# A fused attention and gated MLP kernel on one core: the opening in another order, merged exponentials, and row sums moved to TensorE

## The chip, the core and the metric

The kernel runs on one core of a Trainium2 chip. The metric is device time in microseconds for one execution; the kernel before has been run three times, and the profile is one further execution of it. Five engines with their own instruction streams work side by side: TensorE (PE in the profile, with PEld for its weight loads), VectorE (DVE), ScalarE (ACT), GpSimd (POOL) and SyncE (SP). Each takes its own instructions strictly in the order in which the program lists them. POOL and SP also issue most of the DMA transfers, each into a queue of its own: POOL's is q0 in the profile ("software_dynamic"), SP's is q1 ("hardware_dynamic").

## What is computed

Eight batches of eight heads, 576 positions of 64 values each, go through attention with a mask: a position sees its neighbours within 32 places, and eight global positions see and are seen by all. The result, as 4608 tokens of 512, goes through an MLP whose gate is h times cos(h).

```python
mask = np.abs(pos[:, None] - pos[None, :]) <= window          # window = 32
mask = mask | is_global[:, None] | is_global[None, :]
scores = np.where(mask, scale * (q @ k.T), -1e9)
attn = softmax(scores); x = attn @ v                          # per head
...
h = x @ w_in                                                  # 4608x512 @ 512x2048
out = (h * np.cos(h)) @ w_out                                 # 2048x512
```

## The kernel before, in words

Work comes in **pairs** of heads, 32 of them, four to a batch. The first ten pairs (0 to 9) take a road of their own, called the opening here; the other 22 run in a steady rhythm between MLP work.

For a pair of the opening, steps named by one letter are called in the order of a string, `FRONT`:

- `k`, `q` (`local_k`, `local_q`, L620 and L632): PE transposes the natural keys and queries of the pair (16 matmuls each, helper `turned`, L609, L618), and ACT copies them to fp16 (L627, L638, L639). For the first four pairs PE also picks out the global rows (L323) and ACT copies those (L324). Ahead of `q`, from pair 2 on, stand two filler matmuls that keep PE occupied (L613).
- `s` (`scores5`, L644): PE multiplies keys and queries, ten matmuls into four PSUM banks (L654). ACT takes the exponential of each head: two of 128x488 (L657) and two of 128x384 (L661). DVE multiplies by the mask: two products of 488 columns (L658) and one that covers both heads' 384 (L662).
- `p` (`values5`, L664): PE multiplies weights and values, 20 matmuls with 65 columns (L669); the 65th column is the sum of the weights. The eight global rows come out in four partial sums. DVE adds the four partial denominators (L683), takes reciprocals (L684, L685) and scales (L689).
- `x` (`turn_x5`, L692): five transposes on PE (L701) and three copies or sums on DVE (L702, L705, L707), the last of which adds the four partial global rows. After every fourth pair POOL spreads the global rows (L710).

Other letters of the string are transfers and preparations. `L` loads keys and queries of two pairs (POOL's queue, L290). `M` loads the values of two pairs (SP's queue, L384 and L389), and `C` casts them on POOL (L423). `W` loads one quarter of the first MLP matrix (512 KB, L993, POOL's queue), `O` the second matrix (L997). `E`, `A` gather global rows, `H`, `g` spread them, `y` puts the global value rows into the values, `I` numbers rows and reads the indices into registers, `Z0` to `Z4` build the mask of the steady pairs on DVE (`build_mask`, L448 to L480), `w` and `f` are fillers on PE (L330, L514).

After `FRONT` comes `MID`, a string of the same kind: `1` is one MLP input unit (four 128x512 matmuls on PE, L788, then a cosine on ACT, L794, and a product on DVE, L795), `2` one MLP output unit (four matmuls, L892), `m` and `t` are the two halves of `1`. In `MID` stand the mask parts, the gathers for the later batches and the squares of `n`. Strings `FIFTH`, `SIXTH`, `ORDER` and `TAIL` then carry the steady part and the end.

PSUM has eight banks: two for `pv`, two with tag "h" (transposes, MLP units), three with tag "s" and one with tag "o" (scores, outputs).

Of the kernel before, what the change touches and what calls it, by code (L numbers as in the profile page):

```python
# [19 lines left out]
P = 128  # L20
# [33 lines left out]
MID = ("+ 1 1 1 1 Z0 1 1 1 Z5 B5 1 Z1 1 1 Z2 1 1 A0 1 Z3 1 1 A1 1 n0 A2 g10 g11 1 Z4 N K6 1 1 1 1 1 1 1 2 2 kc qc n1 2 2 1 1 B6 2 2 n2 kd qd - 2 2")  # L54
# [5 lines left out]
FRONT = ("M1 s0 E0 C0 E1 L2 w6 k1 q1 L3 w4 s1 M2 M3 y0.0 f8 k2 q2 C1 H0 I p0 y0.1 s2 k3 q3 x0 p1 H1 s3 g4 g5 g6 L4 C2 g7 k4 q4 x1 p2 M4 s4 "  # L60
         "k5 q5 x2 p3 s5 g8 g9 C3 W0 W1 W2 W3 k6 q6 x3 p4 s6 C4 k7 q7 x4 p5 s7 k8 q8 x5 p6 s8 H2 O k9 q9 p7 x6 s9 "
         "x7 p8 m m x8 K5 p9 t t + m m t t x9 -")
# [149 lines left out]
def kernel(  # L212
# [28 lines left out]
    gidx_row = const.tile([1, 2 * G], I32)  # L241
# [4 lines left out]
    nc.sync.dma_start(gidx_row, dview(gi, 0, (2 * G, 1), (1, 2 * G)))  # L246
# [7 lines left out]
    xT = keep.tile([P, NC, NT + 40], FP16)  # L254

# [70 lines left out]
    def warm(n, tag="s"):  # L326

        t = ps.tile([P, 4, P], FP32, tag=tag, bufs=2 + (tag == "s"))
        for _ in range(n):
            nc.tensor.matmul(t, ones16, view(ones16, (0, 4), (1, P)), start=True, stop=True)  # L330
# [76 lines left out]

    def hold_mask(_):

        nc.gpsimd.tensor_copy(gate, mask[0:1, 0, 0:1])  # L410
# [8 lines left out]
    def cast_vn(s):  # L419
        if s == 2:  # L420
            nc.gpsimd.tensor_copy(gate, pm_of[max(pm_of)][0:1, 2 * CN - 1 : 2 * CN])
# [3 lines left out]
    def value_rows(s, part):  # L425

        hs = slice(2 * part, 2 * part + 2)
        rows = ps.tile([P, 512], FP32, tag="h", bufs=2, name="rows")
# [143 lines left out]
    def turn_globals(half, both):  # L572
        t = ps.tile([P, 2, 16 * G], FP16, tag="s" if half else "h", bufs=2 + half)
# [35 lines left out]
    def turned(src, pr, n, ahead=0):  # L609

        bank = ps.tile([P, 512], FP32, tag="h", bufs=2, name="bank")
        for _ in range(ahead):
            nc.tensor.matmul(bank, ones16, view(ones16, (0, 4), (1, P)), start=True, stop=True)  # L613
        t = view(bank.bitcast(FP16), (QP, RW), (1, QP))
# [4 lines left out]
        return t, bank[:, 400 : 400 + G]  # L619
# [24 lines left out]
    def scores5(pr):  # L644
        kp, qp = k5(pr), qb[pr % NK].rearrange("p j c -> p (j c)")
        pm = pm_of[pr] = work.tile([P, 2 * CN], FP16, tag="pm", name="pm")
        tags = (("s", 3), ("s", 3), ("s", 3), ("o", 1))
        st = [ps.tile([P, 512], FP32, tag=tag, bufs=bufs, name="st") for tag, bufs in tags]
        for t in (0, 1, 4, 2, 3):
            i, c = (0, OFF[t]) if OFF[t] < CA else (2, OFF[t] - CA)  # L650
            q0 = 0 if t == 0 else P * t - D
            for h in range(2):
                hp = slice(h * D, (h + 1) * D)
                nc.tensor.matmul(st[i + h][:, c : c + WID[t]], kp[hp, t], qp[hp, q0 : q0 + WID[t]], start=True, stop=True)  # L654
        for h in range(2):
# [538 lines left out]
```

## Time and profile before

| | |
|---|---|
| three runs, us | 336.43, 337.12, 337.4 (median 337.12) |
| profiled execution, span from first to last instruction, us | 335.3 |
| granted TensorE clock, mean | 0.994 |
| busy in the span, us: PE, DVE, ACT, POOL | 322.3, 269.7, 241.1, 107.6 |

The profiled execution's own time is known by its span alone: 335.3 us, which is 1.8 us below the median of the runs and 1.1 to 2.1 us below each of them. What is worked out against the span is carried over to the median with that 1.8 us added. In the rows of a timeline the first number is the start in microseconds from the span's start, the second how long the row lasts, and a bracket gives the idle time before it and what ended that. The first matmul of the steady pairs starts at 82.78 us, and the first long row of MLP matmuls at 52.90 us.

### The profile page before, as it was taken

What the parts mean: (1) busy time and instruction counts of PE and PEld (TensorE: products, weight loads), DVE (VectorE), ACT (ScalarE), POOL (GpSimd) and SP (SyncE); (2) the same over time, 40 slices, a digit from 0 to 9 for tenths busy, and PEclk for the clock granted to TensorE, in tenths of its full rate; (3) what the DMA queues carried; (4) which work ended last, traced back from release to release, by engine and by line L of the source; (5) the groups of instructions that cost most, each with busy time, mean ns of one, the idle gap of its engine ahead of it and who ended that gap; (6) DMA issues with size and microseconds to landing.
All of it is one profiled execution on the core that took longest, in us unless ns stands there. A gap on an engine that the chain in (4) does not pass through costs nothing.

```text
span 335.3 us, 8640 instructions
## 1 busy us (share of the span) xinstructions
PE 322.3 (96%) x3269; PEld 180.1 (54%) x3269; DVE 269.7 (80%) x649; ACT 241.1 (72%) x422; POOL 107.6 (32%) x216
## 2 busy tenths in 40 slices
PE   7999889999999999999999999999999999999992
PEld 3566654444545454545454545454545566666781
DVE  6778889984679798989898989898989878778771
ACT  4788886785958887777778787878787865665710
POOL 7856578361071407241623252325000200000000
PEclk9999999999999999999999999999999999999997
DMA  5999899999999999999999999999990010100212
GB/s 72 213 179 208 152 205 199 194 133 164 138 179 153 150 161 145 201 155 170 147 195 147 164 149 183 135 178 141 194 109 34 32 33 31 65 32 0 96 47 88
DMA packets 167220, 45.01 MB, mean 134 GB/s; under 512 B 153108, under 2 KB 163732, under 8 KB 166996
## 3 DMA queue, kind: packets, MB, share of 16 engines
q1 hardware_dynamic: 107556, 26.73, 55.9%
q0 software_dynamic: 59472, 17.54, 51.0%
q8 instruction: 27, 0.44, 0.6%
q14 instruction: 21, 0.17, 0.2%
q10 hardware_dynamic: 144, 0.13, 0.1%
HBM read 44.93 MB, written 19.17 MB: 191 GB/s over the span
## 4 chain that ended last, share of the span: by engine, by line
PE 84%; DVE 7%; ACT 5%; issue 2%; ACTq 0%; DVEq 0%
PE ph L788 29%; PE po L892 23%; PE wx L852 6%; PE wy L852 5%; PE units L788 4%; PE pv L742 3%; PE t L330 3%; PE st L722 3%; DVE g L795 2%; PE pv L669 2%; PE tx L767 2%; PE bank L618 2%; PE st L654 1%; ACT cos L794 1%; PE bank L613 1%
## 5 line engine op out<-in xcount | busy, mean ns | idle before, releaser
L788 PE MATMUL ph<-xT,w_in 128*128 128x512 f16 x512 | 123.3, 379 | 0.5 <-DVE xg L707 0.2
L794 ACT ACTIVATE cos<-ph,pio 128x512 f16<-128x512 f32 x128 | 86.5, 687 | 41.5 <-PE ph L788 39.4
L795 DVE TENSOR_TENSOR g<-cos,ph 128x512 f16<-128x512 f16 x128 | 85.6, 684 | 17.9 <-ACT cos L794 15.9
L892 PE MATMUL po<-w_out,g 128*128 128x512 f16 x384 | 93.5, 379 | 0.0
L788 PEld LDWEIGHTS <-w_in 128*128 128x128 f16 x576 | 53.8, 98 | 57.7 <-issue 1.5
L892 PEld LDWEIGHTS <-g 128*128 128x128 f16 x384 | 36.6, 98 | 43.1
L725 ACT ACTIVATE e<-st 128x512 f16<-128x512 f32 x44 | 23.9, 594 | 8.2 <-PE st L722 8.1
L726 DVE TENSOR_TENSOR pm<-e,mask 128x512 f16<-128x512 f16 x44 | 18.8, 428 | 13.4 <-ACT e L725 12.1
L1079 POOL COPY gate<-xn 1x1 f16<-1x1 f16 x8 | 1.4, 179 | 81.0 <-DVE xn L753 81.0
L775 POOL COPY xT<-xg 128x4 f16 x48 | 15.8, 328 | 32.2 <-DVE xT L770 29.6
L281 POOL DMA_DIRECT2D q<-in_q_dram x11 | 24.3, 2206 | 0.0
L753 DVE TENSOR_TENSOR xn<-pv,r_all 128x768 f16<-128x768 f32 x22 | 21.1, 958 | 0.7
L852 PEld LDWEIGHTS <-g 128*128 128x128 f16 x192 | 18.7, 98 | 5.2
L914 ACT ACTIVATE xn<-xn 128x1536 f16<-128x1536 f16 (+1 forms) x15 | 21.2, 1411 | 0.0
L281 POOL DMA_DIRECT2D k<-in_k_dram x11 | 18.0, 1638 | 1.4 <-issue 1.4
L794 ACT ACTIVATE cos<-units,pio 128x512 f16<-128x512 f32 x16 | 11.0, 689 | 9.8 <-PE units L788 9.6
L795 DVE TENSOR_TENSOR g<-cos,units 128x512 f16<-128x512 f16 x16 | 11.0, 686 | 7.4 <-ACT cos L794 7.3
L788 PE MATMUL units<-xT,w_in 128*128 128x512 f16 x64 | 16.4, 379 | 0.0
L794 ACT ACT_TABLE_LOAD x12 | 15.4, 1283 | 0.2
L600 POOL COPY kw<-kgT 128x88 f16<-128x88 f16 x22 | 14.6, 884 | 0.0
L725 ACT ACT_TABLE_LOAD x11 | 14.1, 1283 | 0.2
L722 PEld LDWEIGHTS <-kw 64*128 64x128 f16 x484 | 8.4, 95 | 10.2 <-issue 8.4
(215 smaller groups left out, 500.1 us busy)
## 6 DMA issues: line engine op xcount, KB each, us to landing
out_dram<-o SPq DMA_DIRECT2D x24, 256.0 KB
vw<-v SPq DMA_DIRECT2D x32, 165.0 KB
k<-in_k_dram POOLq DMA_DIRECT2D x11, 288.0 KB, 8.1
q<-in_q_dram POOLq DMA_DIRECT2D x11, 288.0 KB, 11.0
v<-in_v_dram POOLq DMA_DIRECT2D x11, 288.0 KB, 5.4
vn<-in_v_dram SPq DMA_DIRECT2D x20, 120.0 KB
w_in<-in_moe_w_in_dram POOLq DMA_DIRECT2D x4, 512.0 KB, 10.1
w_out<-in_moe_w_out_dram POOLq DMA_DIRECT2D x1, 2048.0 KB, 17.8
```

The lines of the kernel that those rows point to most:

```text
L281: nc.gpsimd.dma_start(dst[s].rearrange("t (h d) -> t h d", h=4), dview(src, base, (D, S), (S * D, 4), (1, D)))
L722: nc.tensor.matmul(st[j // 8 * 2 + h][:, j % 8 * C : j % 8 * C + C], kp[hp, j], qp[hp, j], start=True, stop=True)
L725: nc.scalar.activation(e[:, 0:512], st[h], AF.Exp, scale=scale)
L726: nc.vector.tensor_tensor(view(pm[:, h], (1, 512)), e[:, 0:512], view(mask, (1, 512)), ALU.mult)
L753: nc.vector.tensor_tensor(view(xn, (384, 2), (D, 6), (1, D)), view(pv, (512, 2), (65, 6), (1, D)), view(rp, (6, 2), (1, 6), (0, D)), ALU.mult)
L775: nc.gpsimd.tensor_copy(xT[:, :, bass.ds(pool_idx[g] + b * S, 1)], xg[:, :, g : g + 1])
L788: nc.tensor.matmul(ph, w_in16[:, j, f * P : (f + 1) * P], xT[:, j, t * TT : (t + 1) * TT], start=(j == 0), stop=(j == NC - 1))
L794: nc.scalar.activation(cos, ph, AF.Sin, bias=pio2)
L795: nc.vector.tensor_tensor(g, cos, ph, ALU.mult)
L852: nc.tensor.matmul(bank[:, a], left(f)[:, a * P : a * P + P], right(f), start=name in "125" and f == 0 and (split or a == 0), stop=f == HF ...
L892: nc.tensor.matmul(po, g16[:, f, s * P : (s + 1) * P], w_out16[:, f], start=(f == 0), stop=(f == NF - 1))
L914: nc.scalar.activation(view(xn, (BP * P, 2), (1, n)), view(xn, (BP * P, 2), (1, n)), AF.Square, accum_out=x_sq[:, s : s + 1])
```

## The change

Seven edits:

1. **Order.** `FRONT` and `MID` become one string, `OPEN`. The 30 input units and 8 output units that lie ahead of the steady part are the same in number. `k1` and `q1` now stand ahead of `s0`, `k4` ahead of `s3`, `k6` ahead of `s4`, `k8` ahead of `s7`. The mask parts `Z0` to `Z4` stand among pairs 0 to 3. `W3` and `W0` stand ahead of `L4`, `W1` and `W2` behind it. Input units begin behind `s9` and stand between the last `p` and `x` steps.
2. **PSUM.** During the opening the four banks of "s" and "o" are two buffers of two banks (`two_banks`). At the step `F` that pool is closed and one with the old tags is opened.
3. **One exponential and one mask product for both heads.** A pair has two exponentials (2x488 and 2x384) in place of four and two products in place of three.
4. **Global rows.** Six more matmuls per pair add the partial sums inside PSUM; the DVE sum L683, the second reciprocal L685 are gone, and L707 becomes a copy.
5. **Fillers.** The four matmuls between `k0` and `q0` are gone.
6. **Cosine.** Its bias is a constant in the instruction and no longer a column in SBUF.
7. **Small ones.** One index load is gone, the flag at the end borrows another buffer and gets a memset.

```diff
-MID = ("+ 1 1 1 1 Z0 1 1 1 Z5 B5 1 Z1 1 1 Z2 1 1 A0 1 Z3 1 1 A1 1 n0 A2 g10 g11 1 Z4 N K6 ...
+OPEN = ("E0 M1 C0 f8 I M2 Z0 k1 q1 E1 M3 s0 L2 L3 w6 k2 y0.0 Z1 s1 H0 W3 q2 R1 Z2 p0 y0.1 w4 W0 Z3 s2 q3 H2 k3 x0.1 "
+        "P0 p1 k4 H1 R2 C1 g4 L4 Z4 s3 g5 g7 g6 C2 q4 M4 k5 x1.1 p2 k6 s4 q5 p3 x2 s5 g8 q6 x3 g9 W1 N0 C3 - p4 s6 k7 "
+        "q7 A0 W2 C4 O K5 g10 x4.1 p5 k8 s7 k9 q8 x5.1 + p6 g11 s8 q9 p7 x6 s9 m p8 F 1 1 x7.1 1 t K6 p9 1 Q8 m x8.1 "
...
-FRONT = ("M1 s0 E0 C0 E1 L2 w6 k1 q1 L3 w4 s1 M2 M3 y0.0 f8 k2 q2 C1 H0 I p0 y0.1 s2 k3 q3 x0 p1 H1 s3 g4 g5 g6 L4 C2 ...
...
+    def two_banks():
+        return rooms[1].tile([P, 2, 512], FP32, tag="a", bufs=2, name="two")
+    def later_banks():
+        rooms[0].close()
+        rooms[1] = es.enter_context(tc.tile_pool(name="later", bufs=1, space=PSUM))
...
-        for h in range(2):
-            e = work.tile([P, 2 * CB], FP16, tag="e", bufs=3)
-            nc.scalar.activation(e[:, 0:CA], st[h][:, 0:CA], AF.Exp, scale=scale)
-            nc.vector.tensor_tensor(pm[:, h * CN : h * CN + CA], e[:, 0:CA], mask5[:, 0:CA], ALU.mult)
...
+        for i, c, n in ((0, 0, CA), (1, CA, CB)):
+            e = work.tile([P, 2 * CA], FP16, tag="e", bufs=3)
+            if both:
+                nc.scalar.activation(view(e, (n, 2), (1, n)), st[i][:, :, 0:n], AF.Exp, scale=scale)
...
+            nc.vector.tensor_tensor(view(pm[:, c:], (CN, 2), (1, n)), view(e, (n, 2), (1, n)), view(mask5[:, c:], (0, 2), (1, n)), ALU.mult)
...
-        for h in range(2):
-            add(h, 0, P, G, 1, 0, False, True)
+        for t in (4, 2, 3, 0):
+            for h in range(2):
+                add(h, t, D if t else P, G, 1, 0, False, t == 0)
...
-        dg = work.tile([G, 2], FP32, tag="dg")
-        nc.vector.tensor_reduce(dg, view(pv[0:G, :, X + D : X + D + 1], (512, 2), (X, 4)), AX.X, ALU.add)
-        nc.vector.reciprocal(view(rp[0:G, 1:], (NK5, 2), (1, 4)), view(dg, (1, 2), (0, 4)))
...
-        nc.scalar.activation(cos, ph, AF.Sin, bias=pio2)
+        nc.scalar.activation(cos, ph, AF.Sin, bias=pi / 2.0)
...
-        warm(4)
         local_q(0)
```

On ACT, at the first two pairs, the program before has the exponentials of pair 0 (L657, L661) directly behind the copies of its queries (qb), and the copies of pair 1 behind them:

```order
L639 COPY qb_100<-bank 128x5x120
L657 ACTIVATE e<-st 128x488 x2
L661 ACTIVATE e<-st 128x384 x2
L324 CAST kw_97<-bank 128x5x8
L627 COPY kw_97<-bank 128x5x120
L324 CAST qb_101<-bank 128x4x8
```

The changed program has at the same place, with other line numbers (L663 is the copy of queries, L683 the exponential):

```order
L663 COPY qb_101<-bank 128x5x120
L346 CAST kw_98<-bank 128x5x8
L651 COPY kw_98<-bank 128x5x120
L346 CAST qb_102<-bank 128x4x8
L662 COPY qb_102<-bank 128x8
L663 COPY qb_102<-bank 128x5x120
L683 ACTIVATE e<-two 128x976
```

The copies of pair 1 have moved ahead of the exponentials of pair 0, and two exponentials of one head have become one of both.

On POOL, around the load of the last two opening pairs (room_88 and room_90, step `L4`), the program before reads:

```order
L290 DMA room_88<-in_k_dram 80x4x512
L290 DMA room_90<-in_q_dram 80x4x512
L421 COPY gate<-pm 1x1
L423 CAST vw_94<-vn_118 128x20x64
L598 COPY kw_99<-kgT 128x5x8
L605 COPY qb_103<-qgT 128x4x8
L598 COPY kw_96<-kgT 128x5x8
L605 COPY qb_100<-qgT 128x4x8
L598 COPY kw_97<-kgT 128x5x8
L605 COPY qb_101<-qgT 128x4x8
L423 CAST vw_95<-vn_118 128x20x64
L993 DMA w_in_133<-in_moe_w_in_dram 128x4x512 x4
```

The changed program reads there (room_89 and room_91 are what `L4` loads now, the first two rows belong to `L3`):

```order
L312 DMA room_88<-in_k_dram 80x4x512
L312 DMA room_90<-in_q_dram 80x4x512
L577 CAST g_600<-kg_106 128x128
L577 CAST g_602<-qg_105 128x128
L1016 DMA w_in_134<-in_moe_w_in_dram 128x4x512 x2
L582 CAST vg_117<-vg_107 128x128
L432 COPY gate<-pm 1x1
L447 CAST vw_94<-vn_118 128x20x64
L622 COPY kw_97<-kgT 128x5x8
L629 COPY qb_101<-qgT 128x4x8
L312 DMA room_89<-in_k_dram 80x4x512
L312 DMA room_91<-in_q_dram 80x4x512
```

Two quarters of the first MLP matrix now go into POOL's queue ahead of the last keys and queries; before, all four followed them and a cast of values.

147 lines of the change are left out of this document (79 added, 68 removed), and 2 rows, old and new, of the table OPEN.

## Prediction

> **What bounds the kernel now.** I read the page first, for who is busy and on what the end hangs.
>
> ```profile
> PE 322.3 (96%) x3269; PEld 180.1 (54%) x3269; DVE 269.7 (80%) x649; ACT 241.1 (72%) x422; POOL 107.6 (32%) x216
> PE   7999889999999999999999999999999999999992
> DMA  5999899999999999999999999999990010100212
> PE 84%; DVE 7%; ACT 5%; issue 2%; ACTq 0%; DVEq 0%
> ```
>
> PE is busy for 96% of the span and carries 84% of the chain that ended last. So time can be gained only where PE idles or does useless work, and the second line shows that this is in the first slices; 13.0 us of the span are idle in all. The DMA engines are full from the second slice to the thirtieth, which will matter for a rival.
>
> Then the table of busy time by stage, for four stretches that I chose at the score matmuls of pairs 0, 3 and 9, at the first long row of MLP matmuls (52.90), and at the first steady pair (82.78). Columns are the stretch, its length, and the busy time of PE, PEld, DVE, ACT, POOL.
>
> ```profile
> 10.60:24.19 13.59, 13.17 (x312) 9.35 (x311) 9.22 (x26) 10.74 (x30) 10.31 (x14) 1.00 1.16 195
> 24.19:45.25 21.06, 18.95 (x418) 13.70 (x414) 18.45 (x60) 17.98 (x43) 13.51 (x30) 1.00 1.06 185
> 44.84:52.90 8.06, 7.25 (x81) 4.24 (x81) 6.89 (x23) 5.16 (x8) 5.86 (x14) 1.00 1.24 202
> 52.90:82.78 29.88, 29.84 (x140) 13.10 (x137) 24.79 (x59) 21.92 (x33) 13.87 (x20) 1.00 1.56 171
> ```
>
> Pairs 3 to 9 take 21.06 us, 3.51 each, and PE idles for 2.1 us of it. The stretch behind pair 9 has 0.8 us of idle, the one to 82.78 almost none. The granted clock is 1.00 throughout. Last, the timeline of one pair in the middle, PE and ACT.
>
> ```profile
> 30.99 0.55 PE L654 MATMUL st<-qb,kw 64*128 64x136 f16 x10 [0.38 <-issue]
> 31.39 1.05 ACT L657 ACTIVATE e<-st 128x488 f16<-128x488 f32 x2 [0.50 <-PE st L654]
> 31.47 0.47 PE L618 MATMUL bank<-ident,room 75*64 75x75 f16 x16
> 31.87 0.61 PE L613 MATMUL bank<-ones 128*128 128x512 f16 x2
> 32.33 0.88 ACT L661 ACTIVATE e<-st 128x384 f16<-128x384 f32 x2
> 32.41 0.47 PE L618 MATMUL bank<-ident,room 76*64 76x76 f16 x16
> 32.81 0.45 PE L701 MATMUL tx<-ident,xn 128*128 128x128 f16 x5
> 33.07 0.69 ACT L627 COPY kw<-bank 128x600 f16<-128x600 f16 x1
> 33.10 1.03 PE L669 MATMUL pv<-vw,pm 128*128 128x65 f16 x20
> 33.66 0.73 ACT L639 COPY qb<-bank 128x600 f16<-128x600 f16 x1
> 34.44 0.55 PE L654 MATMUL st<-qb,kw 64*128 64x136 f16 x10 [0.31 <-ACT qb L639]
> ```
>
> Read by starts, the loop is this: ACT does the exponentials from 31.39 to 33.07, then both copies until 34.39; the next scores wait for the copy of the queries, and ACT idles 0.50 us until they are there. That is the ring of ACT and one PE step. But PE is nearly as full: scores 0.48, keys 0.40, two fillers 0.54, queries 0.40, transposes 0.29, values about 0.95 (20 matmuls, their row less its tail), together 3.06 of 3.45 us.
>
> **The change part by part.** A unit is four 128x512 matmuls. For its price, and for the fillers, I take a row of the chain of waits and the row of four early fillers. Beside them stand the marks of the first pairs.
>
> ```profile
> 9.63 1.04 PE L330 MATMUL t<-ones 128*128 128x512 f16 x4
> 18.08 0.47 PE L618 MATMUL bank<-ident,room 76*64 76x76 f16 x16
> 18.71 1.04 PE L669 MATMUL pv<-vw,pm 128*128 128x65 f16 x20
> 19.59 0.45 PE L430 MATMUL rows<-vw,one_v 128*8 128x128 f16 x5
> 19.97 0.55 PE L654 MATMUL st<-qb,kw 64*128 64x136 f16 x10
> 23.78 0.55 PE L654 MATMUL st<-qb,kw 64*128 64x136 f16 x10
> 101.93 0.86 PE po L892 x4
> room<-in_q_dram POOLq DMA_DIRECT2D x1, 320.0 KB, 8.1
> ```
>
> *Six more matmuls per pair.* 20 take 0.95 us by starts, so 0.0475 each and 0.28 per pair. Their weight load has 8 columns, and nothing in the trace says that this would cost more; if the loads were free it would be half, so 0.14 to 0.28. I take 0.28.
>
> *Merged exponentials.* Two of 488 columns take 1.05 us, one alone 0.572, so the second adds 0.48; for 384 it is 0.88, 0.499 and 0.38.
>
> ```profile
> L657 ACT ACTIVATE e<-st 128x488 f16<-128x488 f32 x20 | 10.4, 572 | 4.4 <-PE st L654 4.4
> L661 ACT ACTIVATE e<-st 128x384 f16<-128x384 f32 x20 | 8.8, 499 | 0.0
> L725 ACT ACTIVATE e<-st 128x512 f16<-128x512 f32 x44 | 23.9, 594 | 8.2 <-PE st L722 8.1
> L794 ACT ACTIVATE cos<-ph,pio 128x512 f16<-128x512 f32 x128 | 86.5, 687 | 41.5 <-PE ph L788 39.4 <-DVE xn L753 1.4 <-DVE g L795 0.6
> ```
>
> The slope between them is 73 ns for 104 columns, 0.70 ns each, and 0.92 between 488 and 512. So a merged exponential of 976 takes 0.91 to 1.02 us and saves 0.03 to 0.14; I take 0.07, twice per pair. ScalarE then needs about 2.9 us per pair. The Trainium skill, "ScalarE: Activation LUTs", section "What ACT_TABLE_LOAD costs", says that back-to-back ACTIVATEs overlap by about 93 ns out of a fixed 186; the second of two would keep 93, and merging would save 0.19 us per pair where I take 0.14. The sum below would be the same, since PE sets the pace there.
>
> *Order of the first pairs, to s3.* The queries of the second load are transposed at 18.08 in both, since that load (8.1 us to landing) is issued at the same place. p0 starts at 18.71 and now costs 0.88 (to the row at 19.59) + 0.28; then come the value rows, 0.38; and four fillers, 0.86, which now stand behind p0 and no longer ahead of s1. The scores of pair 2 start at 21.1, or 20.8 if the transposes start when their load is down; before 19.97. From s2 to s3 PE took 3.81 us without a gap; now 0.28 for p1 and 0.40 for `k4` come in, 4.49. So s3 starts at 25.3 to 25.6 in place of 23.78. The delay of s0 behind `k1`, `q1` is swallowed in it. I take 1.5 us later, with 0.5 to 2.3 as the ends: the low one if the fillers fall into a wait, the high one if ACT, which must copy `k4` first, is late too.
>
> *Pairs 3 to 9.* By PE rows a pair costs 3.06 + 0.28 = 3.34, six make 20.04, and since `k4` is done already 0.40 goes: 19.6 in place of 21.06, a gain of 1.5. ACT allows it: 2.9 per pair, and 0.5 of waiting in four of the six (`k` stands between `q` and `s` in the others), 19.4 in all. By the busy time of the table it is 18.95 + 1.7 - 0.4 = 20.2, a gain of 0.8 at most if no idle is left. Ends: 0.4 to 1.8.
>
> *Behind s9.* From 44.84 to 52.90 PE did s9, two values steps, three transposes and four units: 0.48 + 1.90 + 0.87 + 3.44 = 6.7 of 8.06 us, so 1.37 were lost to waits. In the new order a unit stands behind s9, three more before p9, and more behind. Their cosines wait for the table switch, but by then five banks can take units. I take all 1.37 as filled, less two values steps at 0.28: a gain of 0.8, ends 0 and 1.37.
>
> *Mask parts.* They leave the stretch to 82.78. It holds 26 input and 8 output units, 34 x 0.86 = 29.2 of 29.88 us. So 0 to 0.6 can go, and I take 0.3. In the opening they lie on DVE, whose busy time is 9.22 of 13.59 us there.
>
> *Cosine without the column.* 687 against 594 ns for the exponential of the same shape: 0.09 less, 144 times. ACT waits for PE there (39.4 us in the row), so the 13 us are hidden; 0.1 comes through at a table switch, ends 0 to 0.4.
>
> *At nothing:* the three small DVE operations per pair (DVE waits in every pair); the four fillers gone at 8.0, as PE then waits for the first queries anyway; the memset at the end. If their cover goes, the fillers cost 0.9 and the DVE operations 0.3 per pair.
>
> Sum: + 1.5 - 1.5 - 0.8 - 0.3 - 0.1 = - 1.2 us. The span goes from 335.3 to 334.1; with the 1.8 us that lie around it, **335.9 us** against 337.12. This kernel's runs tell about 0.3%, 1.0 us, from no change.
>
> **The rivals.** *Transfers late, slower.* `W3` and `W0`, 1.05 MB, now stand in q0 ahead of the last keys and queries, which `k8` transposes and PE waits for in order. Below: the two queues' packets, MB and share from 20 to 25 us, then from 30 to 35, the cast that waited for values, the old place of the weights, and their size beside that of the values (four rows of 120 KB and one of 96 to a load).
>
> ```profile
> q0 software_dynamic: 908, 0.88, 108.9%
> q1 hardware_dynamic: 276, 0.09, 11.0%
> ...
> q0 software_dynamic: 494, 0.47, 59.2%
> q1 hardware_dynamic: 2134, 0.55, 58.5%
> ...
> 36.94 1.43 POOL L423 CAST vw<-vn 128x1280 f16<-128x1280 f32 x1 [3.83 <-DMA vn<-vg]
> 38.31 3.00 POOL L993 DMA_DIRECT2D w_in<-in_moe_w_in_dram  x4
> w_in<-in_moe_w_in_dram POOLq DMA_DIRECT2D x4, 512.0 KB, 10.1
> vn<-in_v_dram SPq DMA_DIRECT2D x20, 120.0 KB
> vn<-in_v_dram SPq DMA_DIRECT2D x5, 96.0 KB
> ```
>
> Both queues together move 0.97 to 1.02 MB in 5 us, 0.2 MB per us, and that is their limit. From about 18 us on the changed kernel must move two loads of keys and queries and the last (0.655 MB each), two loads of values (0.59 each), the two quarters, and small gathers: 4.2 MB, 21 us, so they are down at about 39. `k8` comes at about 38.1 (s3 at 25.3, then 12.8 by the PE rows). If the values of the fifth load (0.59 MB) mix in, it is 43. So the wait lies between 0 and 4.9; at its middle, 2.5, the result is 335.9 + 2.5 = 338.4. A landing at 39.3 takes the gain away, and past 40.3 the kernel is slower by more than a measurement's bound. For it speaks the full DMA row; against it, that the old kernel left the DMA half idle at 35 to 40 us, and that the cast at 36.94 waited for values, not for keys. The Trainium skill, "DMA: Bandwidth & Descriptors", section "Queues, rings and completion order", has each engine take turns between queues, a packet at a time. The equal shares from 30 to 35 us agree, those from 20 to 25 don't; by turns the weights would hold up the keys behind them in their own queue most, as this rival has it.
>
> *No change.* The first pairs lose the high end, 2.3, and the stretch behind s9 gains only half, 0.4: 2.3 - 1.5 - 0.4 - 0.3 - 0.1 = 0.0, 337.1. For it: PE was without a gap from s2 to s3, so all that is put there costs in full. That one exponential for two doesn't do what it says belongs here: ACT's rows show next to no fixed cost between neighbours.
>
> *Faster than forecast.* The first pairs lose 0.5 only, the later terms come at - 1.8, - 1.0, - 0.5 and - 0.2: - 3.0, 334.1. Against it speaks that PE's own work grows by 60 matmuls.
>
> **How the numbers follow.** The forecast has a chance of 0.36, the faster case 0.12, no change 0.25, late transfers 0.27. The first two make faster by over 0.3%: 0.48; same 0.25; slower 0.27. The range reaches from 333.5, a little under the fast case, to 339.2: the upper third of the late transfers, 0.09, lies beyond it, and a few hundredths below. Faster and slower cases hold three quarters between them, so the forecast's own range: 335.1 to 336.5.
>
> **What would show it.** Right: s3 starts near 25.3, s9 near 44.9; from s9 to the steady part PE has no idle; the first steady scores come at about 81.6 and all behind it shifts with them. Merged exponentials near 0.97 and 0.82 us, cosines near 594 ns, 26 matmuls of values per pair near 1.23 us by starts. Wrong: an idle PE ahead of `k8`'s transposes or ahead of a values step with a DMA as the releaser; s9 past 46; or a steady part that takes another time than 16.65 us per two pairs, which no term here has.

## The result, and the profile after

The changed kernel takes 345.03 us (median of 4 runs, 344.27 to 348.61), the kernel before 337.26 on the same chip (4 runs, 336.43 to 337.55). The ratio is 1.0239, with a 95% interval of 1.0203 to 1.0276: slower by about 8 us, where 1.2 us faster was forecast. A ratio leaves out executions that lie over 1.5 per cent above the fastest of their kernel, so what happens in some executions only shows in the list of a kernel's times and not in its ratio.

The profiled execution took 344.27 us, its span is 342.6. First the page: busy time, the granted clock in 40 slices, the DMA's share, and the chain of work that ended last.

```profile
PE 326.7 (95%) x3325; PEld 184.3 (54%) x3325; DVE 266.7 (78%) x620; ACT 226.9 (66%) x402; POOL 106.2 (31%) x216
PEclk9699989999999999999999999999999999999999
DMA  5999979999999999999999999999993000200213
PE 68%; DMA 19%; SPq 4%; DVE 3%; ACT 3%; issue 1%; POOL 1%; ACTq 0%
```

Two things are new. In the second slice the clock falls, and 19% of the chain are DMA transfers, where none stood in that line before. Then the four stretches at the new marks (s0 14.27, s3 27.06, s9 50.77, long row 59.32, first steady scores 90.49); the last three columns are the granted clock, the DMA's share and GB/s:

```profile
14.27:27.06 12.79, 12.79 (x261) 8.06 (x258) 8.17 (x25) 9.76 (x22) 8.36 (x13) 0.87 0.98 180
27.06:50.77 23.71, 21.09 (x438) 15.36 (x436) 18.02 (x42) 17.32 (x30) 14.86 (x32) 0.93 1.05 178
50.77:59.32 8.55, 8.55 (x99) 5.23 (x98) 7.99 (x20) 5.92 (x9) 7.01 (x17) 1.00 1.18 181
59.32:90.49 31.17, 28.16 (x137) 12.71 (x135) 19.52 (x44) 18.03 (x31) 8.16 (x11) 1.00 1.63 133
```

The third row is as forecast, PE busy throughout. The others are not: the first two have a clock below 1, the second has 2.6 us of idle PE and the last 3.0, where the kernel before had 0.04. By the marks the changed kernel is 3.3 us late at s3, 5.9 at s9 and 7.7 at the first steady scores; from there to the end of the span it takes 252.1 us, the kernel before 252.5. The loss is all in the opening, in three places.

**The start.** PE's rows around the first scores:

```profile
8.54 0.47 PE L642 MATMUL bank<-ident,room 76*64 76x76 f16 x16 [0.40 <-DMA room<-in_q_dram]
9.17 1.04 PE L352 MATMUL two<-ones 128*128 128x512 f16 x4
10.99 1.39 PE L538 MATMUL pv<-ones 128*128 128x184 f16 x8 [0.79 <-DVE pv L1060]
14.27 0.91 PE L679 MATMUL two<-qb,kw 64*128 64x136 f16 x10
15.11 2.69 PE L352 MATMUL bank<-ones 128*128 128x512 f16 x6
```

Four fillers take 1.04 us at 9.17, but six take 2.69 at 15.11, which is half speed, and the scores 0.91 where they took 0.55. Two waits stand ahead of that: for the first queries, where the removed fillers stood, and for a memset ahead of `f8`. The two stretches at half clock, as rows of the table by stage:

```profile
10.80:17.62 6.82, 6.63 (x88) 4.19 (x87) 2.88 (x12) 3.16 (x7) 3.59 (x6) 0.50 1.10 209
44.92:48.33 3.41, 3.41 (x53) 2.75 (x47) 2.10 (x6) 1.00 (x3) 2.95 (x4) 0.50 0.81 155
```

**The values of pairs 6 and 7.** The third cast of values (`C3`, L447) waits for its load, the values step of pair 6 behind it on PE comes late, and it runs at half clock (1.92 us in place of 1.22). Before, `C3` stood at 36.94. In this trace PE's own idle there, 1.25 us, stands ahead of the keys of pair 9 and is put down to "issue"; that `C3` sets the time is read from the runs below.

```profile
43.91 1.33 POOL L447 CAST vw<-vn 128x1280 f16<-128x1280 f32 x1 [1.86 <-DMA vn<-in_v_dram]
45.57 1.92 PE L694 MATMUL pv<-vw,pm 128*128 128x65 f16 x26
```

**The copy of the keys of pairs 10 and 11.** The transposing load of these keys (`kT`) ends only at 81.9. VectorE waits 6.12 us for it, the MLP's products (`g`, L816) stand behind it on VectorE, and PE waits for them.

```profile
67.28 14.58 DMA kT<-k
81.88 0.97 DVE L654 COPY kw<-kT 128x1320 f16<-128x1320 f16 x2 [6.12 <-DMA kT<-k]
83.49 5.34 PE L809 MATMUL bank<-xT,w_in 128*128 128x512 f16 x24 [3.01 <-DVE g L816]
```

### The profile page after: what moved, and what is told of

Its sections match the earlier page's. It is cut to its first block, busy times and chain, and to the rows that moved or that the text cites. A ratio compares the mean times of both kernels' runs of the same rounds, so it can differ in the third digit from the quotient of the medians.

```text
span 342.6 us, 8683 instructions
## 1 busy us (share of the span) xinstructions
PE 326.7 (95%) x3325; PEld 184.3 (54%) x3325; DVE 266.7 (78%) x620; ACT 226.9 (66%) x402; POOL 106.2 (31%) x216
## 3 DMA queue, kind: packets, MB, share of 16 engines
HBM read 44.93 MB, written 19.17 MB: 187 GB/s over the span
## 4 chain that ended last, share of the span: by engine, by line
PE 68%; DMA 19%; SPq 4%; DVE 3%; ACT 3%; issue 1%; POOL 1%; ACTq 0%
PE bank L809 25%; PE bank L913 19%; PE bank L873 11%; DMA vn<-in_v_dram 6%; DMA k<-in_k_dram 5%; DMA kT<-k 4%; PE units L809 4%; PE pv L763 3%; PE bank L743 2%; DMA vw<-vg 2%; PE bank L788 2%; DMA gidx_col<-in_global_idx_dram 1%; SPq L406 1%; SPq L390 1%; SPq L459 1%
## 5 line engine op out<-in xcount | busy, mean ns | idle before, releaser
L809 PE MATMUL bank<-xT,w_in 128*128 128x512 f16 x512 | 123.9, 379 | 3.3 <-DVE g L816 3.0
L815 ACT ACTIVATE cos<-bank 128x512 f16<-128x512 f32 x128 | 74.8, 596 | 54.7 <-PE bank L809 50.6
L816 DVE TENSOR_TENSOR g<-cos,bank 128x512 f16<-128x512 f16 x128 | 85.8, 685 | 19.3 <-ACT cos L815 16.5
L913 PE MATMUL bank<-w_out,g 128*128 128x512 f16 x384 | 93.8, 379 | 0.0
L746 ACT ACTIVATE e<-bank 128x512 f16<-128x512 f32 x44 | 23.9, 596 | 8.7 <-PE bank L743 8.6
L774 DVE TENSOR_TENSOR xn<-pv,r_all 128x768 f16<-128x768 f32 x22 | 21.1, 958 | 0.7
L683 ACT ACTIVATE e<-two 128x976 f16<-128x976 f32 (+1 forms) x20 | 16.9, 898 | 5.2 <-PE two L679 5.2
L687 DVE TENSOR_TENSOR pm<-e,qT 128x976 f16<-128x976 f16 (+1 forms) x20 | 13.8, 702 | 6.7 <-ACT e L683 6.4
L815 ACT ACTIVATE cos<-units 128x512 f16<-128x512 f32 x16 | 9.6, 599 | 11.4 <-PE units L809 11.0
L654 DVE COPY kw<-kT 128x1320 f16<-128x1320 f16 x22 | 12.0, 551 | 6.1 <-DMA kT<-k 6.1
L816 DVE TENSOR_TENSOR g<-cos,units 128x512 f16<-128x512 f16 x16 | 11.0, 686 | 7.5 <-ACT cos L815 7.3
```

The costliest lines, as they stand in the source:

```text
L683: nc.scalar.activation(view(e, (n, 2), (1, n)), st[i][:, :, 0:n], AF.Exp, scale=scale)
L746: nc.scalar.activation(e[:, 0:512], st[h], AF.Exp, scale=scale)
L774: nc.vector.tensor_tensor(view(xn, (384, 2), (D, 6), (1, D)), view(pv, (512, 2), (65, 6), (1, D)), view(rp, (6, 2), (1, 6), (0, D)), ALU.mult)
L809: nc.tensor.matmul(ph, w_in16[:, j, f * P : (f + 1) * P], xT[:, j, t * TT : (t + 1) * TT], start=(j == 0), stop=(j == NC - 1))
L815: nc.scalar.activation(cos, ph, AF.Sin, bias=pi / 2.0)
L816: nc.vector.tensor_tensor(g, cos, ph, ALU.mult)
```

## The experiments

Three theories: **the clock** (the missing fillers, and `f8` ahead of `s0`), **the weights** (`W3`, `W0` ahead in the first queue, q0, starve the values in the second, q1), and **K6** (the load of pairs 12 and 13 no longer waits behind the gate `N`, as it did in `MID`, and runs beside the transposes). Each has a kernel with that one thing put back, and a rival. The runs lie on several chips, on which the kernel before has medians of 337.3 to 338.4 us, so kernels are compared by their ratios. The marks of all kernels (start of the score matmuls in us, span, and the ratio to the kernel before on the same chip with its interval):

| kernel | s0 | s3 | s9 | first steady | span | ratio |
|---|---|---|---|---|---|---|
| before | 10.61 | 23.78 | 44.84 | 82.78 | 335.3 | 1 |
| changed | 14.27 | 27.06 | 50.77 | 90.49 | 342.6 | 1.0239 (1.0203 to 1.0276) |
| e1_fill4 | 13.59 | 25.91 | 50.62 | 90.52 | 341.2 | 1.0128 (1.0096 to 1.016) |
| e2_weights_late | 13.38 | 26.19 | 47.55 | 91.85 | 343.2 | 1.0161 (1.0091 to 1.0231) |
| e3_k6_late | 13.70 | 25.96 | 51.48 | 88.03 | 340.6 | 1.009 (1.0056 to 1.0123) |
| e4_k10_late | 14.30 | 30.88 | 52.81 | 91.38 | 344.9 | 1.0108 (1.0067 to 1.0149) |
| e5_three | 13.58 | 25.86 | 47.85 | 85.18 | 336.7 | 1.0027 (0.9988 to 1.0067) |
| e6_code_old_order | 10.51 | 23.92 | 44.93 | 83.71 | 335.0 | 0.9957 (0.9925 to 0.9989) |
| e7_no_ahead | 10.56 | 23.21 | 43.42 | 82.24 | 334.7 | 0.9921 (0.9899 to 0.9944) |
| e8_before_no_fill | 11.28 | 29.60 | 50.67 | 88.79 | 341.0 | 1.0014 (0.998 to 1.0048) |
| e9_before_no_row | 10.81 | 24.86 | 46.29 | 84.62 | 336.2 | 0.9993 (0.995 to 1.0036) |
| e10_three_no_ahead | 12.89 | 25.35 | 47.55 | 85.90 | 337.3 | 1.0063 (1.0027 to 1.0099) |
| e11_front_mid | 10.67 | 23.33 | 45.84 | 89.17 | 340.4 | 1.008 (1.0043 to 1.0117) |
| e12_before_no_ahead | 10.57 | 23.31 | 45.26 | 83.19 | 335.2 | 0.9987 (0.9957 to 1.0016) |

### The fillers back

```diff
         local_k(0)
+        warm(4)
         local_q(0)
```

> The changed kernel with one thing put back: the four filler matmuls between the first keys and the first queries (0.9 us of PE work at about 8.0 us). Theory that the opening's loss of 3.5 us is the clock (the fillers' absence and the wait for the memset of the values' ones column leave PE idle for 0.5 and 0.8 us, and the granted clock then reads 0.50 from 11.0 to 17.5 us): PEclk 1.0 throughout 10 to 20 us, the first score matmul (14.27 us now) at 11 to 12 us, the first steady scores (90.49 us now) near 87.5, and the time 3 us shorter, 341 to 343 us. Rival, that the first queries' load rules the start and the fillers are worth nothing: first scores at 14.0 to 14.5, time within 0.5 us of the changed kernel's 345. A third way: the gap of 0.8 us at 10.2 stays and halves the clock by itself, then the first scores stay at 14 as well, but with the idle at 8.0 gone.

Measured: 343.05 us. The clock is 1.00 from 10 to 20 us, and s3 comes at 25.91 in place of 27.06; s0 only at 13.59, not 11 to 12 and nearer to the rival's 14.0 to 14.5. Yet s9 and the first steady scores stand where they stood, because the values of pairs 6 and 7 end the wait at the same time as ever:

```profile
43.98 1.25 POOL L447 CAST vw<-vn 128x1280 f16<-128x1280 f32 x1 [3.23 <-DMA vn<-in_v_dram]
45.28 1.21 PE L694 MATMUL pv<-vw,pm 128*128 128x65 f16 x26 [1.01 <-POOL vw L447]
```

The 1.2 us won at s3 are waited away at `C3` and in shorter waits about it (0.27 to 0.74 us). By its ratio the kernel gains 1.1 per cent on the changed one all the same; in this profile a gain appears only behind the marks (span less first steady scores 250.7 in place of 252.1).

### The weights behind the values

```diff
-s1 H0 W3 q2 ... y0.1 w4 W0 Z3 ... x3 g9 W1 N0 C3 - p4 s6 k7 q7 A0 W2 C4
+s1 H0 q2 ... y0.1 w4 Z3 ... x3 g9 N0 C3 W0 W1 W2 W3 - p4 s6 k7 q7 A0 C4
```

> The changed kernel with the casts of the first matrix's four parts, W0 to W3, directly behind the values' third cast C3, as in the kernel before; nothing else is moved. Theory that W3 and W0, let go at 23 us, fill the first queue and starve the third values' load in the second queue (issued by 33.3 us, down at 43.9): C3 starts before 42.0 instead of 43.91, the idle of 1.25 us ahead of the k9 row goes, the granted clock does not fall at 45, the scores of pair 8 follow those of pair 7 after 3.6 to 4.0 us (5.66 now), and the time is 1.5 to 2.5 us shorter. Rival, that the first layer's own loads (L3 and the four-wide L4) starve it, whatever the matrix does: C3 within 0.5 us of 43.9, time within 0.5 us. It may be worse for the long MLP row, whose weights now come later: then PE shows waits for the weights between 50 and 80 us.

Measured: 344.9 us (4 runs). The marks came as the theory said, and so did the wait for weights; the shorter time isn't clear. `C3` starts at 40.70 in place of 43.91, no wait is left ahead of p6, and s9 comes 3.2 us earlier, at 47.55. The ratio is 1.0161 after 1.0239, but the two intervals overlap, and in the trace all is given back behind s9:

```profile
40.70 1.25 POOL L443 CAST vw<-vn 128x1280 f16<-128x1280 f32 x1
67.08 1.89 PE L909 MATMUL bank<-w_out,g 128*128 128x512 f16 x8 [1.45 <-DMA w_out<-in_moe_w_out_dram]
83.16 7.03 PE L805 MATMUL bank<-xT,w_in 128*128 128x512 f16 x24 [3.84 <-DVE g L812]
```

The output weights now come later, and the keys of pairs 10 and 11 come when they came, so whoever is earlier only waits longer for them.

### K6 behind a gate

```diff
+    def hold_gate(f):
+        nc.gpsimd.tensor_copy(gate, g_of[1][0:1, f, 0:1])
...
-1 t K6 p9 ... n1 1 1 1 2 2 2 B6
+1 t p9 ... n1 1 1 1 Y1 K6 2 2 2 B6
```

(`Y` calls `hold_gate`.)

> The changed kernel with the load K6 put back behind a gate that opens only late in the long row (just ahead of the last values' part), where the kernel before had it behind its N gate. Theory that K6's bytes in the first queue at 60 to 71 us slow the transposes of the keys of pairs 10 and 11 (14.58 us each pair of DMAs, landing at 81.9), on which VectorE stands with the g products behind it: kT lands by 78 us, VectorE's copies no longer wait 6.12 us, PE's idle of 3.01 us ahead of the output matmuls at 83.5 goes to 0.5 or less, and the time is 2 to 3 us shorter. Rival, that the keys' copies merely stand too early in VectorE's order: the wait for kT shrinks by less than 3 us, the idle at 83 us stays over 1.5 us and the time gains less than 1.5 us. K6 later may itself be late for the steady part: then a wait of PE for values of pairs behind 10 appears after 95 us.

Measured: 341.38 us. From s9 to the first steady scores it takes 36.55 us in place of 39.72, and no PE wait stands at 83 us. `kT` is copied at 76.39 without a wait. The two queues in the 5 us from 70 to 75, when the transposes run (packets, MB, share), of the changed kernel:

```profile
q0 software_dynamic: 3293, 0.55, 150.5%
q1 hardware_dynamic: 918, 0.24, 45.7%
```

and of this one:

```profile
q1 hardware_dynamic: 3912, 0.76, 107.9%
q0 software_dynamic: 8, 0.01, 0.4%
```

With K6 held, q0 is empty and the transposes in q1 move three times the bytes. From 65 to 70 us the two kernels differ little: q1 moves nothing in the changed one and 0.05 MB here, beside a full q0 in both (205.9% and 184.1% of the engines' time).

### The keys 10 and 11 behind the output matmuls

```diff
-2 + 1 k10 k11 A2 1 1 n2 2 1 1 q10 q11
+2 + 1 A2 1 1 n2 2 1 1 k10 k11 q10 q11
```

> The changed kernel with the two steps k10 and k11 moved to directly ahead of q10 and q11, behind the output matmuls of the long row; the loads stay where they are. Theory that VectorE's order is what costs (the copies of the keys stand ahead of the g products that the output matmuls need): the idle of 3.01 us at 83.5 us goes, the first steady scores (90.49 now) come at 87.5 to 88.5 and the time is 2 to 3 us shorter. Rival, that the transposes' lateness by itself sets the start of the steady part: the wait moves behind the outputs, the first steady scores stay within 1 us of 90.5, and the time gains less than 1 us.

Measured: 343.38 us. Its profiled execution was disturbed at 20 us (a wait of 2.8 us of PE and 6.8 us at half clock, of which the table shows the trace at s3), so only the stretch behind s9 is compared: 38.57 us, between the 39.72 of the changed kernel and the 36.55 of K6 held. 1.85 us of PE's wait stay:

```profile
87.83 1.89 PE L805 MATMUL bank<-xT,w_in 128*128 128x512 f16 x8 [1.85 <-DVE g L812]
```

By this one profile, the slowest of the ten executions, moving the step wins 1.15 of the 3.17 us that holding K6 wins. The ratios of the two kernels, 1.0108 and 1.009, can't be told apart, so how the loss divides between the place and the lateness of `kT` is open. With `kT` in time, as in e3_k6_late, the place costs PE nothing.

### All three

> The changed kernel with three things put back at once: the four fillers between the first keys and the first queries, W0 to W3 directly behind C3, and K6 behind a gate that opens late in the long row. The three theories (clock at 10 to 20 us, values starved by W3 and W0, kT slowed by K6) say together where the marks lie if each loss is its own: first scores at 13.4 (one by one they lay at 13.4 to 13.7 with the clock at full speed), s3 at 25.9, s9 at 47.5, first steady scores at 84.1 (36.6 us behind s9, as with K6 late alone), time 337 to 338.5, so about that of the kernel before; the loss of 8 us is then these three. Rival, that they are one and the same queueing that moves from place to place: a wait of over 1 us comes up elsewhere (values of pair 8 to 9, the output weights at 67 us) and the time stays over 340.

Measured: 338.72 us, a ratio of 1.0027, from which 1 can't be told apart (interval 0.9988 to 1.0067): the loss is these three, up to what that interval leaves. Its stretches:

```profile
13.58:25.86 12.28, 11.60 (x263) 7.81 (x259) 8.57 (x26) 10.19 (x23) 7.20 (x14) 1.00 0.90 165
25.86:47.85 21.99, 19.72 (x436) 14.42 (x435) 17.12 (x42) 17.21 (x30) 14.86 (x33) 1.00 0.94 168
47.85:56.00 8.15, 8.15 (x91) 4.92 (x91) 7.58 (x18) 5.78 (x8) 7.87 (x14) 1.00 1.24 209
56.00:85.18 29.18, 28.57 (x140) 12.97 (x139) 21.16 (x44) 18.17 (x32) 9.84 (x15) 1.00 1.49 171
```

The clock is 1.00 throughout, and from s9 on the stretch is 37.33 us long, 0.6 under the kernel before. What it still loses stands ahead of s9. There is also the answer to how the weights starve the values. Between 25 and 40 us, first the changed kernel, then, behind it, this one:

```profile
q0 software_dynamic: 2362, 2.32, 91.3%
q1 hardware_dynamic: 2290, 0.59, 28.8%
```

```profile
q0 software_dynamic: 1497, 1.45, 57.9%
q1 hardware_dynamic: 5953, 1.51, 50.4%
```

While both queues have work, they move the same number of packets (2362 and 2290), but a packet of q0 holds 0.98 KB on average and one of q1 0.26. So q1 gets a fifth of the bytes, as long as q0 is full. The Trainium skill, "DMA: Bandwidth & Descriptors", section "Queues, rings and completion order", says that an engine takes turns between queues packet by packet; these counts agree with it. The prediction reckoned one common rate for both queues, and it read the equal shares of time from 30 to 35 us (59.2% and 58.5%) as turns, where the packets of its rows are 494 and 2134.

### The edits of the code in the old order

`OPEN` is filled with the steps of `FRONT` and `MID` (with `R1`, `P0`, `F`, `R2` and `Q8` where the old code set the same states), and the four fillers are back.

> The changed kernel's code (merged exp and mask product in the first ten pairs, global rows summed by TensorE, cosine bias without its column, pool of two-bank tiles) with the order of steps of the kernel before, fillers included. Theory that the order alone costs, and that the code edits give what was forecast for them (pairs 3 to 9 about 1.0 to 1.5 us shorter, nothing lost in the first pairs): first scores at 10.6, s3 near 23.8, s9 at 43.3 to 44.0 (44.84 in the kernel before), first steady scores at 81 to 82, time 335 to 336.5, faster than the kernel before by about 1 us. Rival, that the code edits are worth nothing or cost (four single banks of scores become two pairs of banks, so the next pair's scores wait for the one wide exp): s3 to s9 at 21 us or more and the time equal to or over that of the kernel before.

Measured: 336.75 us, ratio 0.9957, so the edits of the code alone make the kernel faster, by 0.1 to 0.8 per cent. The expectation was wrong about where: s3 to s9 takes 21.01 us, as before and as its rival had it. One pair, PE's rows of its trace:

```profile
34.32 0.55 PE L675 MATMUL two<-qb,kw 64*128 64x136 f16 x10
34.80 0.47 PE L638 MATMUL bank<-ident,room 75*64 75x75 f16 x16
35.20 0.60 PE L633 MATMUL bank<-ones 128*128 128x512 f16 x2
35.74 0.47 PE L638 MATMUL bank<-ident,room 76*64 76x76 f16 x16
36.14 0.45 PE L720 MATMUL two<-ident,xn 128*128 128x128 f16 x5
36.43 1.22 PE L690 MATMUL pv<-vw,pm 128*128 128x65 f16 x26
37.72 0.39 PE L675 MATMUL two<-qb,kw 64*128 64x136 f16 x6
```

An undisturbed pair takes 3.34 to 3.40 us, about 0.1 us less than before, and PE has no idle in it. Two disturbed pairs (3.66 us at s3, 3.85 at s7) take up most of what that gives. What this trace shows as gain lies at the very end: behind the issue of the last output write, the span goes on for 6.1 us in the kernel before and 4.6 here.

### The old kernel without the four fillers

> The kernel before, without the four fillers between the first keys and the first queries; nothing else. Theory that their absence is what lets the clock fall: in some or all executions the granted clock reads 0.50 for 3 to 7 us between 9 and 18 us, the mean clock lies at 0.985 to 0.990 instead of 0.994, and the time is 0 to 2 us longer. Rival, that in this order nothing else waits at 10 us and the fillers are free, as the prediction had it: clock 1.0 in the first 30 us, first scores at 10.6 or a little earlier, time within 0.5 us.

Measured: 340.07 us (median of 10). Six executions lie at 337.22 to 340.76 with a mean clock of 0.991 to 0.998, four at 342.77 to 348.27 with 0.962 to 0.980. Of the 24 executions of the kernel before beside it none has a mean clock under 0.987. In the profiled execution, one of the four, the wait for the queries is 0.57 us, and one microsecond later four fillers take 1.82 us in place of 1.04:

```profile
8.58 0.79 PE L618 MATMUL bank<-ident,room 76*64 76x76 f16 x16 [0.57 <-DMA room<-in_q_dram]
9.53 1.82 PE L330 MATMUL t<-ones 128*128 128x512 f16 x4
```

So taking the fillers away costs little or nothing in most executions and 5 to 10 us in the others, also in the old order; the theory had 0 to 2.

### The fillers of each pair

```diff
-            t, g = turned(qn[pr // 2 % NN], pr, QP, 2 if pr > 1 else 0)
+            t, g = turned(qn[pr // 2 % NN], pr, QP)
```

First in the old order with the new code:

> The changed kernel's code in the order of the kernel before (as in the run named e6_code_old_order), without the two filler matmuls that each pair from the third on sets ahead of its queries' transposes (0.54 us from start to start). In that run pairs 5 to 7 stood 3.34 to 3.40 us apart and PE had no idle in them: scores 0.48, keys 0.40, fillers 0.54, queries 0.40, transposes of x 0.29, values 1.22 make 3.33. Theory that the merged exp has moved the bound of these pairs from ScalarE and VectorE to TensorE, where the fillers now cost in full: pairs 2.85 to 3.05 us apart (ScalarE's sum is 2.87), s9 at 42 to 43 in place of 44.93, time 334 to 335.2. Rival, that latency from score to values sets the period and PE's work only fits in: pairs 3.3 apart with idle PE of 0.4 to 0.5 in each, time within 0.5 us. A third way: that idle lets the granted clock fall, with the time 1 to 3 us longer in some executions.

then with the three things put back:

> The changed kernel with fillers, W0 to W3 late and K6 late (as e5_three), and without the two fillers ahead of each pair's queries. Theory as for e7_no_ahead: where the pairs are not held up by the third values or by instruction supply (5 of 9 steps), each is 0.3 to 0.5 us shorter, s9 at 45.8 to 46.5 in place of 47.85, time 1.5 to 2 us under e5_three, so 336 to 337. Rival, that the loads set the pace in this order (values' casts C2 and C3 wait for their loads): s9 within 0.5 us of 47.85 and the time within 0.5 us of e5_three.

and in the kernel before:

> The kernel before, without the two filler matmuls ahead of each pair's queries; nothing else. Theory that the fillers cost only where the merged exp has made PE full: in the old code pairs stand 3.45 to 3.5 us apart with PE idle of 0.3 to 0.4 in each, so their removal leaves s3 to s9 at 20.5 to 21.1 us, time within 0.5 us of the kernel before (or longer, where the clock falls). Rival, that the 0.8 per cent of e7_no_ahead over the kernel before is the fillers' alone: s3 to s9 under 20, time 1.5 us or more shorter.

Measured: e7_no_ahead 335.19 us, ratio 0.9921, the fastest of all. But the theory on the pairs fell. Three pairs of this kernel (first row), and three of the kernel before without and with these fillers:

```profile
30.00:40.08 10.08, 8.36 (x220) 7.12 (x220) 8.35 (x21) 8.61 (x15) 6.45 (x12) 1.00 0.83 163
```

```profile
31.40:41.80 10.40, 7.56 (x201) 6.34 (x202) 9.11 (x31) 8.99 (x21) 6.67 (x13) 1.00 0.80 149
```

```profile
30.99:41.39 10.40, 9.42 (x207) 6.89 (x208) 9.09 (x31) 8.99 (x21) 6.57 (x13) 1.00 0.91 168
```

A pair takes 3.36 us without the fillers and 3.34 to 3.40 with them, and 3.47 in the old code, to the hundredth with or without. PE's idle only grows. In e7_no_ahead the next scores still wait for the copy of the queries:

```profile
40.08 0.55 PE L675 MATMUL two<-qb,kw 64*128 64x136 f16 x10 [0.39 <-ACT qb L659]
```

So what sets the pace is the ring that the prediction saw in the kernel before (exponentials, copies, next scores), and the merged exponentials shorten it by 0.11 us. The gain of e7_no_ahead at s9, 1.5 us over e6_code_old_order, comes from the first pairs (0.7 by s3) and from the two pairs that were disturbed there; whether its time is shorter than that of e6_code_old_order is not settled, as the intervals overlap. In the old code the removal gives nothing, 0.9987 (0.9957 to 1.0016), and it isn't without risk: three of the twelve executions have a mean clock of 0.961 to 0.981 and take 338.12 to 344.88 us.

In the new order it gains nothing: e10_three_no_ahead takes 339.47 us, with s9 at 47.55 as its rival had it. The intervals of 1.0063 and of e5_three's 1.0027 overlap, so a loss in time isn't shown. The clock is, as in the third way named for e7_no_ahead: it is at 0.964 to 0.990 in all nine executions, where e5_three has 0.995 or more in eight of ten. Its trace waits for keys at 24.37 and then runs three stretches of 3.41 us at half clock:

```profile
24.37 0.72 PE L642 MATMUL bank<-ident,w_out 75*64 75x75 f16 x16 [1.38 <-DMA w_out<-in_k_dram]
```

```profile
24.23:34.47 10.24, 9.62 (x162) 7.86 (x163) 5.93 (x14) 6.40 (x11) 5.25 (x13) 0.50 1.21 203
```

### The small load of indices

```diff
-    gidx_row = const.tile([1, 2 * G], I32)
-    nc.sync.dma_start(gidx_row, dview(gi, 0, (2 * G, 1), (1, 2 * G)))
...
-                gidx_row[0:1, 0 : 2 * G : 2], engines=...
+                gidx_all[0:1, 0 : 2 * G : 2], engines=...
```

> The kernel before, without the small load of the indices' row (GpSimd reads the same numbers from the copy on all partitions, as in the changed kernel); nothing else. In the two traces of old code the span ends 6.1 and 5.9 us after the last output write is issued, in six traces of the changed code 4.6 to 4.9. [...] Rival, that the end differs by something else in the code: 5.9 to 6.1 as before, time within 0.4 us.

Measured: 338.09 us, ratio 0.9993. The span ends 5.3 us behind the last issue, between the old and the new code; e12_before_no_ahead, which keeps the load, ends 5.7 behind it. So it isn't shown that this load lengthens the end, and no gain in time can be seen. Why the end is about 1 us shorter with the new code (4.5 to 4.9 us in its ten traces) stays open.

### A version from the best pieces

`OPEN` is the order of e7_no_ahead up to s9 and the changed order behind it, with `Z0` to `Z4`, `A0`, `A1`, `g10`, `g11` and `K5` among the units, and K6 behind its gate.

> A version put together from what the runs so far showed: the changed kernel's code, the order of the kernel before up to the scores of pair 9, without the two fillers ahead of each pair's queries (as e7_no_ahead), and from there the changed kernel's order (x7 to x9 among the first units, keys 10 and 11 ahead of their queries), with the mask parts among the units and K6 behind the late gate. Theory that the best pieces add up, since they stand in different stretches: s9 at 43.4 as in e7_no_ahead, first steady scores 36.6 to 37.3 us behind it (38.8 in e7_no_ahead, 36.55 in e3_k6_late, 37.33 in e5_three), time 333 to 334, a ratio of 0.988 to 0.991 to the kernel before. Rival, that the mask parts, the gathers and the globals of pairs 10 and 11, which the changed order had put into the first pairs, now hold up the units between 46 and 80 us: waits of PE for g there of over 1 us, time 335 or more.

Measured: 341.22 us, the rival's case. s9 comes at 45.84, as the clock falls at 34.85, and from s9 to the first steady scores it takes 43.33 us, the longest but for e2_weights_late. PE waits seven times for products of VectorE:

```profile
45.84:89.17 43.33, 38.32 (x229) 17.93 (x228) 31.61 (x75) 24.18 (x39) 17.72 (x30) 1.00 1.42 175
PE bank L809 <- DVE g L816: 4.0, 7, 1.2
```

e5_three has the same order there without the mask parts, the gathers, the globals and `K5`, which stand ahead of s9 in it, and takes 37.33 us with no such wait of over 0.3 us. So these steps can't simply stand among the units of this order; which of them holds VectorE up was not tried (the copies of the keys that `K5` brings, at 76.59, wait for no load).

## Why the prediction was wrong, step by step

The steps beside e5_three, in which the three losses are undone, and the changed kernel; each as the change against the kernel before, in us:

| step | forecast | e5_three | changed |
|---|---|---|---|
| first pairs, at s3 | + 1.5 | + 2.1 | + 3.3 |
| pairs 3 to 9 | - 1.5 | + 0.9 | + 2.7 |
| s9 to first steady scores | - 1.1 | - 0.6 | + 1.8 |
| from there to the span's end | - 0.1 | - 1.0 | - 0.4 |
| sum | - 1.2 | + 1.4 | + 7.3 |

**"At nothing: ... the four fillers gone at 8.0, as PE then waits for the first queries anyway"** is the first step that failed. The cover was named rightly, and its price, 0.9, was the wrong kind of price: what the wait costs is the clock. At half clock for 6.82 us the first pairs lose 0.9 to 1.2 us at s3 (27.06 against 26.19 to 25.86), and the clock falls again at 44.9, behind the 1.25 us of idle PE. That fillers in a wait do nothing on the path was true; they kept the granted clock up. Of the five traces without the four fillers, four fall at 9.0 to 10.8 us and e2_weights_late doesn't; of the nine with them none falls ahead of 20 us. What this makes of the 8 us is open: e1_fill4 gets to s9 no earlier, e3_k6_late falls for 3.41 us at 9.03 and still has s3 at 25.96, and no kernel has the weights and K6 put back without the fillers.

**First pairs, + 1.5.** In three traces with the clock at 1.00 there, s3 comes at 25.86, 25.91 and 26.19, 2.1 to 2.4 us late, at or just over the high one of the step's ends (0.5 and 2.3). From s2 to s3 it takes 4.23 us, where 4.49 was forecast after 3.81, so the added work of PE costs there as was said, and less. What is mis-sized is s2, at 21.6 to 22.0 in place of 20.8 to 21.1; why was not traced.

**Pairs 3 to 9, - 1.5.** This failed for two reasons. Some 2.8 us of the changed kernel's 5.9 at s9 are the values of pairs 6 and 7: at full clock and with the same fillers s9 is at 50.62 in e1_fill4 and at 47.85 in e5_three. The rival *Transfers late* had the cause, `W3` and `W0` ahead, and its result of 338.4 was on the right side, but it had `k8` waiting in the same queue, and reckoned both queues at a common rate. The traces show q1 starved: `C3` is 3.2 to 3.4 us later in the kernels of this order with `W3` and `W0` ahead (43.91, 43.98, 43.97; e4_k10_late, disturbed, is left out) than in those without (40.70, 40.56). The second reason is the pace of a pair. An undisturbed pair of the new code takes 3.36 us, near the 3.34 of the sum, though the ring sets it and not PE's rows; but an undisturbed old pair takes 3.47, so 0.11 is won a pair where the step had 0.17 (3.51 to 3.34), beside the keys of `k4`. In the new order, with keys done ahead, the last five pairs of e2_weights_late do come 3.28 us apart (31.14 to 47.55), but s3 to s4 took 4.95 there.

**Behind s9 and mask parts, - 0.8 and - 0.3.** The price was right where the transposes come in time: 37.94 before, 37.33 in e5_three and 36.55 in e3_k6_late, so 0.6 to 1.4 less. What the sum left out is K6. It was issued at 71.4 us, behind the gate `N`, in the kernel before, and at 58.9 now, ahead of the transposes at 67.3; no term priced it, although both strings show it. Behind s9 it cost 3.2 us (39.72 against 36.55), and undone alone it gives the largest gain of the three.

**Cosine, - 0.1; merged exponentials; values.** The sizes hold: cosines 596 ns for 594, the two exponentials 898 ns in the mean for 0.97 and 0.82 us, values 1.22 us for 1.23. The rule of the Trainium skill that was weighed there ("ScalarE: Activation LUTs", section "What ACT_TABLE_LOAD costs") gave 0.19 a pair; the old pair's exponentials take 1.68 us by starts (31.39 to 33.07), the merged ones 1.57 (35.20 to 36.77, one pair), so 0.11 came, nearer to the 0.14 taken from the rows.

**Signs named as wrong** were right: s9 past 46 in the changed kernel, and in e1_fill4 idle PE ahead of a values step, behind a cast that waited for its load. The order, not the code, made the loss: the same code in the old order has a ratio of 0.9957.

## What to carry to other kernels

- An order of steps moves transfers too: list for each queue what is now issued earlier, and ask which load in the *other* queue, with smaller packets, is due at that time. A gate that goes (here `N` ahead of K6) is a change of its own with its own price.
- Fillers in a wait can be worth more than the wait: take them away only where PE's busy share stays high, and look at the granted clock of many executions, not of one.
- Losses in a row hide each other. By the ratios, of the 2.4 per cent lost the fillers give back 1.1, the weights 0.8 and K6 1.5, but all together 2.1, so single gains don't add up; and a repair whose gain isn't clear of the noise (e2_weights_late) may still be needed. Judge each by the marks, not by the time alone.

## What the runs showed of the hardware

The granted clock fell in stretches of 3.41 us or two or three of them (3.41, 6.82, 10.24). The profiled executions of these kernels show eleven such falls up to 53 us, and in the 3.41 us ahead of each PE was busy for 39 to 74% of the time; ahead of the one at 10.80 for 2.41 us, with no single wait over 0.8. In the kernel before no such window from 8 to 80 us is under 83%; e7_no_ahead has one of 66%, e1_fill4 one of 49%, and both kept the clock. So a low share makes a fall possible and doesn't bring it each time. The Trainium skill, "TensorE: Matmul & The Clock Gate", section "Part 1: The HAM clock gate (the "warmup" mystery)", tells of a window of 3413 ns that runs freely; the length agrees. Where in the window a wait falls is not all, though. The falls of the changed kernel, at 10.80 and 44.92, lie ten windows apart, and ten more lead to 79.05; there PE is busy for 42% of a window, and the clock stays at 1.00 behind it:

```profile
79.05:82.46 3.41, 1.43 (x7) 0.56 (x6) 0.58 (x2) 1.21 (x3) 0.00 (x0) 1.00 1.34 80
```

What else decides is open. The Trainium skill, "TensorE: Matmul & The Clock Gate", section "Why this matters for your kernels", names idle gaps of over about 3 us as the danger; here shorter ones were enough, ahead of the fall at 10.80 one of 0.40 and one of 0.79 us.

A wait of 0.8 to 1.0 us in the middle of the values step of pair 2, at 29.6 to 30.8 us, which the profile puts down to "issue", stands in four traces of the changed order (the changed kernel, e1_fill4, e2_weights_late, e5_three). In each of them one packet of the instruction queue q14 stands close to its start (in the half microsecond from 29.7, 28.7, 29.0 and 28.7 us), and so does one ahead of the 1.25 us at pair 9 (from 41.8); but e3_k6_late has one from 28.6 without such a wait. No run was made on it, and its cause is open.
